# A gated mix of a long convolution and a token MLP: the convolution in two halves with a split transform, the shift filter on the matrix engine, one-pass gelu, and a list-scheduled instruction order

## The chip, the cores and the metric

The kernel runs on one core of one Trainium2 chip. A core has engines that run side by side: TensorE for matmuls (PE; its weight loads are PEld), VectorE (DVE), ScalarE (ACT), GpSimd (POOL) and SyncE (SP), which here issues most of the DMA transfers. Each engine takes its instructions in the order given: in the run in stated order below, DVE stood for 51.6 us at one operation with later ones ready behind it. Matmul results land in PSUM, and in both kernels ACT carries them to SBUF, which is called an eviction here.

The metric is the device time of one execution in microseconds. All runs compared below are of the fast state, unless it is said otherwise; executions of one kernel agree within about 1%.

## The reference, cut to what matters

```python
# S = 2048 tokens, D = 640 channels, F = 1536, bf16 inputs
g = sigmoid((q * gate_w).sum(-1))                   # one gate a token
# part A: shift filter of 4 taps, then a causal convolution as long as the sequence
k_shift = sum(k delayed by j tokens * shift_k[:, j] for j in 0..3)
kv = k_shift * v
y  = irfft(rfft(pad(kv)) * rfft(pad(ssm_k)))[:S] + kv * ssm_D
a  = q * y
# part B: MLP over the token axis
h  = layernorm(q)
u  = gelu_tanh(h.T @ w1 + b1)                       # 2048 -> 1536
b  = (u @ w2 + b2).T                                # 1536 -> 2048
return g * a + (1 - g) * b
```

Both MLP products are 2048 x 1536 x 640. They stay 384 matmuls of 320 columns each in both kernels.

## The kernel before: the parts that the argument touches

The convolution is cut into four blocks of 512 tokens. Each block of the filter and of kv is transformed by matmuls with cosine and sine tables, real and imaginary part by itself, and the output spectrum of block m sums the products of all pairs of blocks j and m - j, which makes ten pairs.

```python
def fwd_units(src_tile, blk0, dst_fn, scale):        # 8 units a block
    for c, Tt in ((0, Tc), (1, Ts)):                 # cosine, sine
        for kb in range(NB):                         # 4 frequency tiles
            # ... two PSUM banks, 4 + 4 matmuls of 320 columns, one eviction on ACT

def kv_tile(t, e_="DVE"):                            # shift filter of one tile of 128 tokens
    tt(e_, ka, ks[:, 0, :], shkb[:, 0, :], ALU.mult)
    tt(e_, k0, ks[:, 1, :], shkb[:, 1, :], ALU.mult)
    # ... eight operations of 640 elements in all, on VectorE

def product_pair(j, m_, slot):                       # one of ten pairs, 6 or 8 operations of 2560
    tt(e_, t0, Ar, Wr, ALU.mult)
    tt(e_, t1, As, Ws, ALU.mult)
    tt(e_, Zr, Zr, t0, ALU.add)
    # ...

def b1_set(s_, ...):                                 # gelu by a polynomial and a sigmoid
    evac(ubs[:, fi, :], q0 + fi, ACT.Identity, bias=b1c, scale=1.0)
    evac(sqs[:, fi, :], q0 + fi, ACT.Square, bias=b1cs, scale=GC)
    # ...
    stt(ge, sqf, sqf, 1.0, ubf, ALU.add, ALU.mult)                 # DVE
    gelu_sig.append(lambda ...: act(sgf, sqf, ACT.Sigmoid, scale=GS2))
    gelu_mul.append(lambda ...: tt(ge, gT[...], sgf, ubf, ALU.mult))   # DVE
```

Its order was laid out by hand: shift-filter tiles between the sets of the first MLP product, and the last product pairs between blocks of the second.

Of the kernel before, what the change touches and what calls it, by code (L numbers as in the profile page):

```python
# [17 lines left out]
class _Tracker:  # L18
# [31 lines left out]
    def regions(self, ap):  # L50
# [24 lines left out]
        if outer and nouter <= 64:  # L75
            idxs = [0] * len(outer)
            for _ in range(nouter):
                o = rem
                for (st, ct), i in zip(outer, idxs):
                    o += st * i  # L80
                lo = o
                hi = o
                for st, ct in inner:
                    ext = st * (ct - 1)
                    if ext < 0:
                        lo += ext
                    else:
                        hi += ext
                hi += 1
                assert lo >= 0 and hi <= rowsize, (name, apl, off, rowsize)  # L90
                res.append((space, p0, p1, base + lo * esize, base + hi * esize))
                for d in range(len(outer) - 1, -1, -1):
                    idxs[d] += 1
                    if idxs[d] < outer[d][1]:
                        break
                    idxs[d] = 0
        else:
# [10 lines left out]
            res.append((space, p0, p1, base + lo * esize, base + hi * esize))  # L108
        return res

# [161 lines left out]
    def mm(self, ps_ap, lhsT, rhs, start, stop, final_val):  # L272
        reads = [lhsT, rhs]
        acc_r = []
        for a in reads:
# [9 lines left out]
        ins = self.nc.tensor.matmul(ps_ap, lhsT=lhsT, rhs=rhs, start=start, stop=stop)  # L285
# [3 lines left out]
        if start:  # L289
            for r in ps_regs:  # L290
                self.add_record(r, "W", src)
        if stop:
# [7 lines left out]
def _chunks(D, maxc=512):  # L300
    n = (D + maxc - 1) // maxc
    base = D // n
    rem = D % n
    out = []
    lo = 0
    for i in range(n):
        w = base + (1 if i < rem else 0)
        out.append((lo, w))
        lo += w
    return out  # L310
# [12 lines left out]
NASP = 4  # L323
NUB = 4
NEPI = 7
KV_PRE = 3
KV_CHUNKS = (3, 3, 3, 2, 2, 0)
TM_PAIR_US = 9.5
TM_PAIR0_US = 7.0
TM_BLOCK_PE_US = 8.8  # L330
TM_PH4_LAG_US = -5.0
TM_EPI_US = 0.8
TM_EPI_LAG_BLOCKS = 2
EPI_ENG = "DVE"
OUT_ENG = "SP"


def _build(nc, A_q, A_k, A_v, A_shift_k, A_ssm_k, A_ssm_D, B_x, B_w1, B_b1, B_w2, B_b2, gate_w, out):
    Bsz, S, D = A_q.shape
    assert Bsz == 1  # L340
    F = B_w1.shape[1]
    KS = A_shift_k.shape[1]
    assert KS == 4
    P = 4
    n = S // P
    assert n % 128 == 0 and S % 128 == 0 and F % 128 == 0
    NB = n // 128
    NT = S // 128
    FT = F // 128
    L = 2 * n - 1  # L350
    N2 = 2 * n
    IB = 2 * NB
    DCH = _chunks(D, 512)
    NDC = len(DCH)
    assert NDC <= 2
    FS = 2 if FT % 2 == 0 else 1
    NSETS = FT // FS

    xd = A_q
    kd = A_k  # L360
    vd = A_v

    with ExitStack() as es:
        clk = {}
        for e in ENGS:
            clk[e] = es.enter_context(nc.semaphore(f"clk_{e}"))
        T = _Tracker(nc, clk)

        def dsem(name):
            s = es.enter_context(nc.semaphore(f"d_{name}"))  # L370
            T.add_dma_sem(name, s)

        for nm in ["const", "shk", "b", "out"]:
            dsem(nm)
        for i in range(NT):
            dsem(f"x{i}")
        for i in range(NEPI):
            dsem(f"xe{i}")
        for i in range(2):
            dsem(f"k{i}")  # L380
            dsem(f"v{i}")
            dsem(f"w2{i}")
        for i in range(2):
            for j in range(2):
                dsem(f"w1{i}{j}")
                dsem(f"w1p{i}{j}")
        for i in range(P):
            dsem(f"wT{i}")

        pp = []  # L390
        for i in range(4):
            h = es.enter_context(nc.psum_tensor(f"pp{i}", [128, 1024], F32))
            T.reg_psum(h, nc.lookup_mloc(h).bank)
            pp.append(h)

        def pview(q, widths):
            w = widths[0]
            assert all(x == w for x in widths)
            if len(widths) == 1:
                return pp[q][:, 0:w]  # L400
            return pp[q][:, :].rearrange("p (c f) -> p c f", c=2)[:, :, 0:w]

        base0 = (nc.sbuf_base + 63) // 64 * 64
        top = nc.sbuf_top
        cur = [base0]

        def alloc(name, shape, dtype):
# [3 lines left out]
            off = cur[0]  # L411
            cur[0] = (off + size + 63) // 64 * 64
            assert off + size <= top, f"SBUF overflow allocating {name}: {off}+{size} > {top}"
# [3 lines left out]

        gwb = alloc("gwb", [128, D], BF16)
        stats = alloc("stats", [128, NT, 6 * NDC], F32)
        mv = alloc("mv", [128, NT, 2], F32)  # L420
        rstd = alloc("rstd", [128, NT], F32)
        nbias = alloc("nbias", [128, NT], F32)
        gpre = alloc("gpre", [128, NT], F32)
        gg = alloc("gg", [128, NT], F32)
        omg = alloc("omg", [128, NT], F32)
        c2 = alloc("c2", [128, NT], F32)
        b2f = alloc("b2f", [128, NT], F32)
        b1f = alloc("b1f", [128, FT], F32)
        b1s = alloc("b1s", [128, FT], F32)
        b2t = alloc("b2t", [128, NT], BF16)  # L430
        b1t = alloc("b1t", [128, FT], BF16)
        cst = alloc("cst", [128, 4], F32)
        acol_i = alloc("acol_i", [128, NB], I32)
        acol_f = alloc("acol_f", [128, NB], F32)
        vpe = alloc("vpe", [128, NT], F32)
        Dall = alloc("Dall", [128, D], BF16)
        Tc = alloc("Tc", [128, NB, N2], BF16)
        Ts = alloc("Ts", [128, NB, N2], BF16)
        gT = alloc("gT", [128, FT, D], BF16)
        wT_base = cur[0]  # L440
        wT = alloc("wT", [128, NT, D], BF16)
        kv_base = cur[0]
        kvall = alloc("kvall", [128, NT, D], BF16)
        persist_end = cur[0]
        cur[0] = kv_base
        xb = [alloc(f"xb{i}", [128, D], BF16) for i in range(NT)]
        assert cur[0] <= persist_end
        cur[0] = persist_end

        cur[0] = wT_base  # L450
        w2b = [alloc(f"w2b{i}", [128, FT, 256], BF16) for i in range(2)]
        xe = [alloc(f"xe{i}", [128, D], BF16) for i in range(NEPI)]
        cur[0] = max(cur[0], kv_base)
        o1 = [alloc(f"o1_{i}", [128, D], BF16) for i in range(NEPI)]
        cg = [alloc(f"cg_{i}", [128, D], BF16) for i in range(NEPI)]
        osb = [alloc(f"osb_{i}", [128, D], BF16) for i in range(2)]
        end4 = cur[0]
        union_base = max(persist_end, end4)

        cur[0] = union_base  # L460
        Wsp = alloc("Wsp", [128, P, 2, NB, D], BF16)
        r1_base = cur[0]

        cur[0] = r1_base
        Zsp = alloc("Zsp", [128, P, 2, NB, D], BF16)
        Asp = [alloc(f"Asp{i}", [128, 2, NB, D], BF16) for i in range(NASP)]
        ptmp = [alloc(f"ptmp{i}", [128, NB, D], BF16) for i in range(2)]
        end2 = cur[0]

        cur[0] = r1_base  # L470
        hall_base = cur[0]
        hall = alloc("hall", [128, NT, D], BF16)
        shkb = alloc("shkb", [128, KS, D], BF16)
        kacc = alloc("kacc", [128, D], BF16)
        ktmp = [alloc(f"ktmp{i}", [128, D], BF16) for i in range(2)]
        junk = ktmp[0]
        late_base = cur[0]
        w1b = [alloc(f"w1b{i}", [128, NT, FS * 128], BF16) for i in range(2)]
        kb_ = [alloc(f"kb{i}", [128, KS, D], BF16) for i in range(2)]
        vb = [alloc(f"vb{i}", [128, D], BF16) for i in range(2)]  # L480
        ub = [alloc(f"ub{i}", [128, FS, D], BF16) for i in range(NUB)]
        save_cur = cur[0]
        cur[0] = cur[0] - (FS * D * 2 + 63) // 64 * 64
        assert KS * D * 2 <= FS * D * 2 or True
        shk2 = alloc("shk2", [128, D, KS], BF16)
        cur[0] = max(save_cur, cur[0])
        gsq = [alloc(f"gsq{i}", [128, FS, D], BF16) for i in range(NUB)]
        NLATE_MAX = 2
        n_early = max(0, NSETS - NLATE_MAX)
        gsg_e = [alloc(f"gsg{i}", [128, FS, D], BF16) for i in range(min(3, NSETS))]  # L490
        gsg = [gsg_e[i % len(gsg_e)] for i in range(NSETS)]
        end1 = cur[0]
        cur[0] = late_base
        brow_i = alloc("brow_i", [128, n], I32)
        prod_h = alloc("prod_h", [128, NB, n], I32)
        tbA = [alloc(f"tbA{i}", [128, NB, 128], I32) for i in range(2)]
        tbB = [alloc(f"tbB{i}", [128, NB, 128], I32) for i in range(2)]
        tbC = [alloc(f"tbC{i}", [128, NB, 128], I32) for i in range(2)]
        tbD = [alloc(f"tbD{i}", [128, NB, 128], F32) for i in range(2)]
        tbE = [alloc(f"tbE{i}", [128, NB, 128], F32) for i in range(2)]  # L500
# [600 lines left out]
```

## Time and profile before

| | before |
|---|---|
| time, median | 293.62 us (3 runs, 292.29 to 295.8) |
| span of the profiled run | 291.6 us |
| PE busy | 247.7 us, 1728 matmuls |
| DVE busy | 239.6 us |
| ACT busy | 113.5 us |

These lines are from the page of the kernel before: busy time by engine with its share of the span, then the busy tenths of PE, DVE and ACT in 40 equal slices (9 is 90% or more), and the shares of the chain of waits that ended last.

```profile
PE 247.7 (85%) x1728; PEld 172.4 (59%) x1728; DVE 239.6 (82%) x375; ACT 113.5 (39%) x153; POOL 35.0 (12%) x72
...
PE   0056989999999999767999999999999999059993
DVE  8999999096699899999999999997269999974211
ACT  2335569981235550746566323222222222002221
...
PE 44%; DVE 40%; DMA 5%; POOL 4%; issue 3%; ACT 3%; ACTq 0%; DVEq 0%; POOLq 0%
```

Neither engine is full over the whole span, but in almost every slice one of them is. That is what a chain of 44% PE and 40% DVE means: they take turns. The table of windows of before names the stages (stretch in us, its length, then busy time of PE, PEld, DVE, ACT and POOL, granted clock, DMA share, GB/s):

```profile
71.00:100.00 29.00, 29.00 (x216) 20.86 (x214) 23.13 (x48) 11.55 (x16) 0.00 (x0) 1.00 0.91 269
100.00:137.00 37.00, 30.12 (x205) 20.13 (x204) 35.86 (x70) 18.54 (x25) 0.00 (x0) 0.95 0.73 214
137.00:205.00 68.00, 68.00 (x490) 48.43 (x489) 65.49 (x57) 26.49 (x37) 0.00 (x0) 0.97 0.14 41
205.00:260.00 55.00, 44.41 (x319) 31.15 (x318) 47.24 (x41) 9.91 (x12) 0.00 (x0) 0.91 0.25 74
260.00:292.00 32.00, 27.18 (x186) 18.69 (x183) 7.33 (x16) 5.83 (x7) 0.00 (x0) 0.93 0.25 81
```

The last row is TensorE alone: 27.2 us of matmuls with DVE busy for 7.3. In the rows before it DVE is busy for 80 to 97% of the time. Two groups of before say with what (engine, operation, tiles, shapes, count, then busy us in total and mean ns of one, then idle time before):

```profile
L506 DVE TENSOR_TENSOR Zsp<-Zsp,ptmp_124 128x2560 bf16<-128x2560 bf16 x16 | 23.8, 1487 | 0.2
...
L506 DVE TENSOR_TENSOR kacc<-kacc,ktmp_128 128x640 bf16<-128x640 bf16 x32 | 15.6, 488 | 0.6
```

The first is part of the pair products, the second part of the shift filter (128 operations of some 0.49 us, 64 us together; the last of the eight for each tile is the product with v).

### The profile page before, as it was taken

What the parts mean: (1) busy time and instruction counts of PE and PEld (TensorE: products, weight loads), DVE (VectorE), ACT (ScalarE), POOL (GpSimd) and SP (SyncE); (2) the same over time, 40 slices, a digit from 0 to 9 for tenths busy, and PEclk for the clock granted to TensorE, in tenths of its full rate; (3) what the DMA queues carried; (4) which work ended last, traced back from release to release, by engine and by line L of the source; (5) the groups of instructions that cost most, each with busy time, mean ns of one, the idle gap of its engine ahead of it and who ended that gap; (6) DMA issues with size and microseconds to landing.
All of it is one profiled execution on the core that took longest, in us unless ns stands there. A gap on an engine that the chain in (4) does not pass through costs nothing.

```text
span 291.6 us, 4373 instructions
## 1 busy us (share of the span) xinstructions
PE 247.7 (85%) x1728; PEld 172.4 (59%) x1728; DVE 239.6 (82%) x375; ACT 113.5 (39%) x153; POOL 35.0 (12%) x72
## 2 busy tenths in 40 slices
PE   0056989999999999767999999999999999059993
PEld 0033657777777776434677777777777776026772
DVE  8999999096699899999999999997269999974211
ACT  2335569981235550746566323222222222002221
POOL 1223988820000000000000000000000000000000
PEclk9997899999999999979899999999999999658999
DMA  6979697347799986692000054002932300016100
GB/s 141 305 145 136 149 164 222 112 143 210 207 287 320 306 259 204 189 276 69 0 2 0 0 169 117 2 0 71 277 118 58 119 3 0 0 44 199 70 22 22
DMA packets 54530, 37.44 MB, mean 128 GB/s; under 512 B 16756, under 2 KB 53870, under 8 KB 54510
## 3 DMA queue, kind: packets, MB, share of 16 engines
q1 hardware_dynamic: 45614, 30.88, 38.2%
q10 hardware_dynamic: 8320, 4.19, 5.3%
q0 software_dynamic: 576, 2.10, 3.5%
q8 instruction: 13, 0.21, 0.3%
q14 instruction: 7, 0.06, 0.1%
HBM read 31.92 MB, written 2.62 MB: 118 GB/s over the span
## 4 chain that ended last, share of the span: by engine, by line
PE 44%; DVE 40%; DMA 5%; POOL 4%; issue 3%; ACT 3%; ACTq 0%; DVEq 0%; POOLq 0%
PE pp L285 44%; DVE Zsp L506 8%; DVE kacc L506 7%; DVE ktmp_128 L506 4%; DVE ptmp_124 L506 3%; DVE ptmp_123 L506 3%; DMA out_dram<-osb_116 3%; DMA kb_132<-in_A_k_dram 2%; DVE ktmp_129 L506 2%; DVE kvall L506 2%; DVE tbC_155 L506 1%; DVE tbC_154 L506 1%; DVE stats L626 1%; DVE gT L506 1%; POOL vpe L511 1%
## 5 line engine op out<-in xcount | busy, mean ns | idle before, releaser
L285 PE MATMUL pp<-Zsp,Tc 128*128 128x320 bf16 x224 | 41.3, 309 | 7.4 <-DVE Zsp L506 7.4
L285 PE MATMUL pp<-Zsp,Ts 128*128 128x320 bf16 x224 | 41.1, 308 | 3.2 <-DVE Zsp L506 3.2
L285 PE MATMUL pp<-wT,Tc 128*128 128x320 bf16 x128 | 21.4, 330 | 20.5 <-DMA wT<-in_A_ssm_k_dram 17.7
L285 PEld LDWEIGHTS pp<-Zsp,Tc 128*128 128x128 bf16 x224 | 22.4, 100 | 17.0 <-DVE Zsp L506 7.7
L285 PEld LDWEIGHTS pp<-Zsp,Ts 128*128 128x128 bf16 x224 | 22.4, 100 | 13.0 <-DVE Zsp L506 3.8
L285 PEld LDWEIGHTS pp<-wT,Tc 128*128 128x128 bf16 x128 | 13.3, 106 | 27.5 <-issue 17.7
L285 PE MATMUL pp<-gT,w2b_93 128*128 128x320 bf16 x192 | 27.2, 300 | 0.0
L285 PE MATMUL pp<-gT,w2b_92 128*128 128x320 bf16 x192 | 27.2, 299 | 0.0
L285 PE MATMUL pp<-hall,w1b_130 128*128 128x320 bf16 x192 | 26.6, 300 | 0.0
L285 PE MATMUL pp<-hall,w1b_131 128*128 128x320 bf16 x192 | 26.6, 299 | 0.0
L546 ACT ACTIVATE Wsp<-pp 128x640 bf16<-128x640 f32 x32 | 21.8, 738 | 8.7 <-PE pp L285 8.5
L285 PE MATMUL pp<-kvall,Ts 128*128 128x320 bf16 x128 | 20.8, 326 | 5.3 <-ACT Asp_119 L546 3.1
L506 DVE TENSOR_TENSOR Zsp<-Zsp,ptmp_124 128x2560 bf16<-128x2560 bf16 x16 | 23.8, 1487 | 0.2
L506 DVE TENSOR_TENSOR Zsp<-Zsp,ptmp_123 128x2560 bf16<-128x2560 bf16 x16 | 23.7, 1484 | 0.0
L285 PEld LDWEIGHTS pp<-gT,w2b_92 128*128 128x128 bf16 x192 | 18.8, 98 | 7.4
L285 PEld LDWEIGHTS pp<-gT,w2b_93 128*128 128x128 bf16 x192 | 18.8, 98 | 7.3
L285 PEld LDWEIGHTS pp<-hall,w1b_130 128*128 128x128 bf16 x192 | 18.8, 98 | 7.3
L285 PEld LDWEIGHTS pp<-hall,w1b_131 128*128 128x128 bf16 x192 | 18.8, 98 | 7.3
L285 PE MATMUL pp<-wT,Ts 128*128 128x320 bf16 x128 | 19.9, 319 | 1.4 <-ACT Wsp L546 1.4
L285 PE MATMUL pp<-kvall,Tc 128*128 128x320 bf16 x128 | 19.3, 309 | 1.6 <-ACT gsq_142 L546 1.5
L285 PEld LDWEIGHTS pp<-kvall,Ts 128*128 128x128 bf16 x128 | 13.2, 105 | 12.2 <-ACT Asp_119 L546 3.8
L285 PEld LDWEIGHTS pp<-wT,Ts 128*128 128x128 bf16 x128 | 13.2, 104 | 7.8 <-ACT Wsp L546 1.8
(198 smaller groups left out, 356.6 us busy)
## 6 DMA issues: line engine op xcount, KB each, us to landing
kb_133<-in_A_k_dram SPq DMA_DIRECT2D x32, 160.0 KB, 2.7
kb_132<-in_A_k_dram SPq DMA_DIRECT2D x29, 160.0 KB
w2b_92<-in_B_w_dram SPq DMA_DIRECT2D x4, 768.0 KB, 4.9
w2b_93<-in_B_w_dram SPq DMA_DIRECT2D x4, 768.0 KB, 5.5
w1b_130<-in_B_w_dram ACTq DMA_DIRECT2D x4, 512.0 KB, 5.9
w1b_131<-in_B_w_dram ACTq DMA_DIRECT2D x4, 512.0 KB, 5.9
vb_134<-in_A_v_dram SPq DMA_DIRECT2D x8, 160.0 KB, 3.6
vb_135<-in_A_v_dram SPq DMA_DIRECT2D x8, 160.0 KB, 3.3
```

The costliest lines, as they stand in the source:

```text
L285: ins = self.nc.tensor.matmul(ps_ap, lhsT=lhsT, rhs=rhs, start=start, stop=stop)
L506: return T.op(eng, lambda e: e.tensor_tensor(out_, in0, in1, op), [in0, in1], [out_])
L511: return e.tensor_scalar(out_, in0, s1, None, op0=op0)
L546: return T.op("ACT", lambda e: e.activation(out_, in_, func, **kw), rr, [out_])
L626: T.op("DVE", (lambda ci, dlo, dw: lambda e: e.bn_stats(stats[:, t, ci * 6:(ci + 1) * 6], xs[:, dlo:dlo + dw]))(ci, dlo, dw), [xs[:, dlo:d ...
```

## The change

The change wants less work on both engines of the chain, and an order that keeps both busy.

- The convolution works on two halves of 1024 tokens. Each half is split by token index modulo 4 into four phases, which are transformed with small tables and then combined on DVE by additions and subtractions (`mixing`, `invmix`). That leaves 256 forward and 128 inverse matmuls where before had 512 and 448, and six large products in place of ten pairs. The filter is loaded as it lies and transposed on TensorE.
- The shift filter is 140 matmuls with diagonal tables (`DG`), on k loaded transposed.
- Gelu is one ACT instruction for a tile.
- The gate's row sums move from DVE to a wide DVE product and 16 ACT sums.
- Every operation is put into a list with an estimated duration, and a list scheduler in the kernel's builder writes the order. At each moment of its model it gives each engine the ready operation that was stated first, or that has a lower priority number.

```diff
-            tt(e_, ka, ks[:, 0, :], shkb[:, 0, :], ALU.mult)      # shift filter: 8 such a tile
+                    for q in range(4):
+                        items.append(((lambda s, b=b, q=q: s[:, 512 * b + 128 * q:512 * b + 512]),
+                                      V(KT[h], base + q, [[4, 128]]), DG[:, db, 0:4 - q, :]..., q == 0, False))
...
-            stt(ge, sqf, sqf, 1.0, ubf, ALU.add, ALU.mult)
-            gelu_sig.append(...); gelu_mul.append(...)
+            act(GT[:, ft, :]..., two, ACT.Gelu_apprx_tanh, bias=b1f[:, ft:ft + 1], vt=vt, prio=0, name="gelu")
...
+        def mixing(R, Th, Ts):                                    # 8 operations of 2560, four times
+            tt("DVE", sl(Th, Ts), sl(R, 0), sl(R, 2), ALU.add)
+            tt("DVE", sl(R, 0), sl(R, 0), sl(R, 2), ALU.subtract)
+            # ...
+        def product(dst, a, v):                                   # six times
+            tt("DVE", P2(T0), P2(a), P2(v), ALU.mult)             # 5120 elements
+            tt("DVE", P2(T1), P2(a), P2(v, True), ALU.mult)
+            tt("DVE", H(dst, 0), H(T0, 0), H(T0, 1), ALU.subtract)
+            tt("DVE", H(dst, 1), H(T1, 0), H(T1, 1), ALU.add)
...
+            tt("DVE", xg[:, :, :], X[:, hk, :, :], V(gwb, 0, [[0, 4], [1, D]]), ALU.mult)
+            for p in range(4):
+                act(xg[:, p, :], xg[:, p, :], ACT.Copy, acc=gpre[:, 4 * hk + p:4 * hk + p + 1], name="ga")
...
-        while pending:                                            # hand-made order
-            j, m_ = pending.pop(0)
-            product_pair(j, m_, j % NASP)
-            emit_ready_quads()
+        y1(0); y1(1)                                              # products of the second half
+        Z1 = invmix(A1[0], A1[1], C3a, None, None)
+        inverse(1, Z1)
+        product(A0[0], A0[0], V0[0])
+        product(A0[1], A0[1], V0[1])
+        Z0 = invmix(A0[0], A0[1], (SS, 0), None, None)
+        inverse(0, Z0)
+        SC.run()                                                  # list scheduling
+        SC.emit()
```

## The prediction

> **What bounds it now.** Busy table: span 291.6 us, PE 247.7 (85%), DVE 239.6 (82%), ACT 113.5. The chain of waits is 44% PE and 40% DVE, in turns. By the table of windows: until 40 us DVE builds tables and statistics while PE waits 17.7 us for the transposed filter; 71 to 137 DVE is nearly full with the shift filter (eight 640-wide operations a tile, 0.49 us each); 137 to 205 both are full; 216 to 259 is pure DVE products (2560 wide, 1.40 to 1.49 us each); 259 to 287 is pure PE (188 matmuls, 28.2 us).
>
> **PE.** Before: 1728 matmuls of 320 columns. After: 1152 (forward 256, MLP 768, inverse 128), 140 shift matmuls (40,960 columns) and 114 small transposes. The trace's dense rate is 137 to 140 ns per 320 columns (224 in 30.6 us; 488 in 68.2 us). Estimates: 1152 x 0.14 = 161; shift 18; transposes 114 x 0.1 = 11. Sum 190 us, some 52 below before's 242 at that rate.
>
> **DVE.** Estimates from 1.40 to 1.49 us per 2560 elements: four forward mixings of eight operations 46; kv, spectrum-merge and gate products 18; products 56; two inverse mixings 23; statistics (0.41 x 32 + 0.2 x 16) 16; tables 8; normalising 5; epilogue (32 x 0.49) 15. Sum about 187 us, 53 below before. Gone are 128 shift operations (63 us), the gelu polynomial and most of the pair products; new are the mixings.
>
> **ACT.** 64 spectrum evictions (0.71 us), 16 filter evictions, 16 gate sums, 12 shift evictions, 12 gelus, 32 in the tail: about 130 us. It should not bind overall, but paces the first 50 us: 0.71 per eviction exceeds 0.56 for its four matmuls. Table loads stay few: the Trainium skill (ScalarE: Activation LUTs, What ACT_TABLE_LOAD costs) gives 1283 ns; the trace has 1283.
>
> **DMA.** 37 MB becomes about 28; transposed loads (about 145 GB/s in their slices, plain ones about 300) now carry k, needed later than the filter was.
>
> **Critical path.** Both engines of the chain lose about 52 us, and the MLP overlaps the DVE chain. Estimated DVE chain: filter spectra mixed near 66, signal spectra 104, products 142, inverse mixing 154, second half 190, then 12 us of inverse matmuls, epilogue and store: about 203. PE: MLP from about 50 us, when weights and normalised x exist, 155 us left: 205. Add 5 to 8% for stalls of a static order, throttled stretches (clock 0.91 to 0.97 late) and the start.
>
> **Prediction:** 220 us, range 203 to 242; faster by over 2% 0.96, within 2% 0.02, slower 0.02.
>
> **Right or wrong shows as:** PE busy 190 to 215, DVE 178 to 195, ACT 120 to 140; PE over 90% busy from 55 us to near the end; DVE gaps under 30 us in total; a final stretch with DVE idle under 15 us (28 before); no wait over 5 us for w1 or v.
>
> **What would make it wrong.** (1) The second MLP product and the shift read weights with element step 4. The skill (TensorE: Matmul & The Clock Gate, Weight-path perf modes) allows fast weight load to a step of 1,024, so I assume no penalty; before has none to compare. If LDWEIGHTS exceeds 140 ns, 384 matmuls lengthen. (2) k transposes delaying v and w1. (3) An order built from estimated durations: head-of-line stalls on PE and ACT. (4) Reversed-half operands losing the [...]rate, adding 30 us or more to DVE.

## The result and the profile after

The kernel after takes 217.03 us (median of 4 runs, 216.88 to 217.26) against 293.08 for before in the same measurements. The ratio is 0.7395, interval 0.7361 to 0.7428. A ratio is the mean time of one kernel's fast runs over that of the other's of the same rounds, so not quite the ratio of the medians. The profile of after:

```profile
PE 192.9 (90%) x1406; PEld 139.7 (65%) x1406; DVE 184.5 (86%) x197; ACT 119.3 (55%) x181; POOL 18.0 (8%) x22
...
PE   0579944999879899999999999999999999999993
DVE  8999599998999258966999999999997669998650
ACT  2798999799984996395213112113314472323751
...
PE 72%; ACT 23%; DMA 2%; issue 0%; DVE 0%
```

PE lost 54.8 us of busy time (247.7 to 192.9), DVE 55.1 (239.6 to 184.5) and ACT gained 5.8. The sum of PE and DVE busy time over the span was 1.67 before and is 1.75 now. The turns are gone: from the 15th slice on PE is full, and DVE is nearly full beside it in most slices. The start has a new owner: ACT holds 23% of the chain, all but 0.9 us of it before 73 us. The table of windows of after (columns as above):

```profile
0.00:73.00 73.00, 54.32 (x385) 36.12 (x386) 66.33 (x105) 61.98 (x104) 18.04 (x22) 0.93 0.73 204
73.00:212.00 139.00, 138.59 (x1022) 103.61 (x1022) 117.64 (x91) 56.76 (x78) 0.00 (x0) 1.00 0.30 98
```

PE is busy for 138.6 of the 139 us from 73 to 212, and for 54.3 of the first 73. Near its end the chain of waits reads so, in order of time (start, duration, what):

```profile
70.81 1.28 ACT L641
72.10 0.80 ACT GT L641
72.91 0.05 issue
72.95 138.65 PE pp L291 x1022
```

One reads "the kernel is PE-bound for two thirds of its span" there. The experiments below show that this is only half of it.

Two smaller readings answer questions of the prediction. These are groups of after: the weight loads of the first MLP product, whose weights lie side by side, and of the second, whose weights are read with an element step of 4; then one of the reversed-half products.

```profile
L291 PEld LDWEIGHTS pp<-X,ring_80 128*128 128x128 bf16 x256 | 24.9, 98 | 11.5 <-issue 1.8 <-ACT C_85 L641 0.2
...
L291 PEld LDWEIGHTS pp<-GT,W_1_99 128*128 128x128 bf16 x192 | 21.7, 113 | 4.4
...
L603 DVE TENSOR_TENSOR tm_101<-C_84,SS 128x5120 bf16<-128x5120 bf16 x1 | 2.8, 2818 | 0.0
```

The step of 4 costs 15 ns a load (113 against 98), and the matmul stream hardly feels it: 128 matmuls of the first product in a row took 17.55 us and 96 of the second 13.20 us, 137 and 138 ns each. The reversed-half products keep the rate of the other operations (5120 elements in 2.82 us, twice the 2560 in 1.41 of back-to-back operations).

One DVE operation stands out. These are the timelines of POOL and of DVE in after, around 10 us (start, duration, engine, what); the later instances of the same DVE operation took 1.48 us each:

```profile
9.67 4.46 POOL L603 TENSOR_TENSOR DG<-ident,shk 128x2560 bf16<-128x2560 bf16 x1 [8.07 <-DMA shk<-in_A_shift_k_dram]
...
10.68 0.44 DVE L790 BATCH_NORM_STATS2 stats<-X 128x6 f32<-128x320 bf16 x1
11.04 4.43 DVE L603 TENSOR_TENSOR xg<-X,gwb 128x2560 bf16<-128x2560 bf16 x1
```

While POOL builds the shift table, the DVE operation with one input runs at its usual 0.44 us, but the one with two inputs ends only 1.3 us after POOL does. The Trainium skill (GPSIMD Engine Reference, 1. Specifications) says that POOL shares its SBUF interfaces with VectorE and names two SBUF inputs as a case of contention. The trace agrees, and gives its size: 3 us here, practically a full stop. The last run shows the other direction too: there a POOL copy of 20 columns took 7.16 us, from 29.56 to 36.72 us, while DVE ran two-input operations end to end until 36.66 us. In after the same copy took 0.60 us.

### The profile page after: what moved, and what is told of

Its sections match the earlier page's. It is cut to its first block, busy times and chain, and to the rows that moved or that the text cites. A ratio compares the mean times of both kernels' runs of the same rounds, so it can differ in the third digit from the quotient of the medians.

```text
span 215.2 us, 3363 instructions
## 1 busy us (share of the span) xinstructions
PE 192.9 (90%) x1406; PEld 139.7 (65%) x1406; DVE 184.5 (86%) x197; ACT 119.3 (55%) x181; POOL 18.0 (8%) x22
## 4 chain that ended last, share of the span: by engine, by line
PE 72%; ACT 23%; DMA 2%; issue 0%; DVE 0%
PE pp L291 72%; ACT xg L641 5%; ACT C_82 L641 4%; ACT C_83 L641 3%; ACT wT L641 3%; DMA ssm<-in_A_ssm_k_dram 2%; ACT FTB L641 2%; ACT L641 2%; ACT ksh_94 L641 2%; ACT GTB L641 1%; ACT C_84 L641 1%; ACT ksh_95 L641 0%; ACT O_100 L641 0%; ACT GT L641 0%; DVE O_100 L603 0%
## 5 line engine op out<-in xcount | busy, mean ns | idle before, releaser
L291 PE MATMUL pp<-X,ring_80 128*128 128x320 bf16 x256 | 35.6, 299 | 1.5 <-ACT ksh_95 L641 1.5
L641 ACT ACTIVATE O_100<-pp,c_66,omg 128x640 bf16<-128x640 f32 x16 | 14.2, 885 | 35.0 <-PE pp L291 35.0
L291 PEld LDWEIGHTS pp<-X,ring_80 128*128 128x128 bf16 x256 | 24.9, 98 | 11.5 <-issue 1.8
L291 PE MATMUL pp<-GT,W_1_99 128*128 128x320 bf16 x192 | 26.9, 299 | 0.0
L291 PE MATMUL pp<-GT,W_0_98 128*128 128x320 bf16 x192 | 26.4, 299 | 0.0
L291 PEld LDWEIGHTS pp<-GT,W_1_99 128*128 128x128 bf16 x192 | 21.7, 113 | 4.4
L291 PEld LDWEIGHTS pp<-GT,W_0_98 128*128 128x128 bf16 x192 | 21.8, 113 | 4.3
L291 PE MATMUL pp<-wT,FTB 128*128 128x320 bf16 x128 | 21.8, 335 | 0.0
L291 PE MATMUL pp<-ident,ssm 128*128 128x128 bf16 x80 | 9.5, 287 | 12.9 <-ACT wT L641 6.8
L291 PEld LDWEIGHTS pp<-wT,FTB 128*128 128x128 bf16 x128 | 12.4, 109 | 9.0 <-ACT C_82 L641 1.9
L291 PE MATMUL pp<-X,ring_81 128*128 128x320 bf16 x128 | 17.7, 299 | 0.0
L291 PEld LDWEIGHTS pp<-X,ring_81 128*128 128x128 bf16 x128 | 12.5, 98 | 4.8
L790 DVE BATCH_NORM_STATS2 stats<-X 128x6 f32<-128x320 bf16 x32 | 13.5, 461 | 0.0
L603 DVE TENSOR_TENSOR C_83<-C_84 128x2560 bf16<-128x2560 bf16 x4 | 5.9, 1490 | 7.2 <-ACT C_84 L641 7.2
L641 ACT ACTIVATE xg<-xg 128x640 bf16<-128x640 bf16 x16 | 11.8, 804 | 0.0
L603 DVE TENSOR_TENSOR C_84<-C_85 128x2560 bf16<-128x2560 bf16 x5 | 7.4, 1490 | 3.8 <-ACT C_85 L641 3.8
```

The costliest lines, as they stand in the source:

```text
L291: ins = self.nc.tensor.matmul(ps_ap, lhsT=lhsT, rhs=rhs, start=start, stop=stop, skip_group_check=True)
L603: return SC.add(eng, d, lambda s: T.op(eng, lambda e: e.tensor_tensor(o, a, b, op), [a, b], [o]), [a, b], [o], prio=prio, name="tt")
L641: return T.op("ACT", lambda e: e.activation(o, src, func, **kw), rr + [src], ww)
L790: SC.add("DVE", 0.42, (lambda o, i: lambda s: T.op("DVE", lambda e: e.bn_stats(o, i), [i], [o]))(o, i), [i], [o])
```

## The experiments

Theory A, which the sums of the prediction and the chain of waits of after suggest: the gain is the work taken off both engines, with the order worth a smaller part; after 73 us PE alone sets the pace. (The prediction itself put the DVE chain at 203 us and PE at 205, two nearly equal paths.) Rival B: the order is the larger part, or DVE binds as much as PE. Ratios to after are formed from two ratios to before; the control run, the kernel after unchanged, gave 217.03 us and 0.7375. Except for the stated orders, every variant of after was list-scheduled anew, so its order can differ beyond the edit shown.

> The kernel after unchanged, as control of this call: 217 us, within 0.5%.

### The same operations in stated order

```diff
-        SC.run()
+        SC.program_order()      # operations as stated, PSUM slots dealt in turn
         SC.emit()
```

> The kernel after, with the same operations issued in the order in which the program states them (convolution, first MLP product, second MLP product, products and inverse) instead of the list-scheduled one; PSUM slots dealt in turn. Theory A (most of the gain is work removed from TensorE and VectorE, the order is worth a smaller part): 230 to 250 us, busy times unchanged at about 193 and 185, PE idle up by 15 to 30 us, mostly in the first 90 us. Rival B (the gain is overlap brought by the list-scheduled order): 265 us or more.

Measured: 274.41 us, ratio to before 0.930 (0.926 to 0.933). The rival's number: with the same operations, the program runs 57 us longer. The run changes the dealing of PSUM slots together with the order. Its mean PE clock was also lower, 0.87 to 0.88 in the fast executions (0.97 to 0.98 in after), so a part of the 57 us can be slower matmuls beside the waits. Its profile fell in a slow execution (span 277.4 us, PE busy 201.7, DVE 189.9), so only its large waits are read here, from its view of waits:

```profile
DVE cgb L611 <- ACT cgb L649: 51.6, 1, 51.6
...
PE pp L291 <- DVE C L611: 25.8, 1, 25.8
```

The first is a wait for an order and not for data. The program states the first inverse transform, with its DVE epilogue, before the last two products. PE reaches that transform only after the whole MLP, so DVE stands for 51.6 us at the epilogue with the products ready behind it. Then it works alone, and PE waits 25.8 us. Three moves of statements, each on top of the one before, test how much of the loss is of this kind.

```diff
 # first move
-        inverse(1, Z1)
         ...
         Z0 = invmix(A0[0], A0[1], (SS, 0), None, None)
+        inverse(1, Z1)
         inverse(0, Z0)
 # second move: m1(ft) is one tile of the first MLP product
         for hk in range(2): kv(hk)
+        for ft in range(4): m1(ft)
         # ... first signal transform, kv(2), kv(3)
+        m1(4); m1(5)
         # ... second signal transform
 # third move: the table DG stated at the start; kv(0), kv(1) stated before the mixing of the second filter half
```

> The program-order variant with one move: the second half's products and inverse mixing are stated before the first inverse transform, so VectorE need not wait for that transform's epilogue, which TensorE reaches only after the whole MLP. In the program-order run VectorE idled 51.6 us there and then worked 36 us alone. Theory A (that one inversion costs the tail): 244 to 254 us, VectorE's idle stretch gone, last matmuls dense. Rival B (the tail is bound otherwise): 268 us or more.

Measured: 245.29 us (0.833). The inversion at the tail cost 29 us, as theory A of this run had it. DVE still idles there for 19.6 us of the 51.6, but PE is full through that time.

> The same with a second move: six of the twelve tiles of the first MLP product stated earlier, four before the first signal transform and two before the second, where TensorE waited for VectorE in the program-order run. Theory A (the rest of the loss of the program order is TensorE idling before the MLP): 218 to 232 us. Rival B (the list-scheduled order wins by many small choices): 238 us or more.

Measured: 234.37 us (0.7965). It gained 11 us and falls between the two theories, 218 to 232 and 238 or more; PE still waited 16.8 us for the table DG, which POOL made late because the operations stated before it waited for DVE.

> The program order with the two moves and a third: the table for the shift filter is stated at the start, and the two gate products of the first half before the mixing of the second filter half, so the first signal transform can start while VectorE mixes. In the run with two moves VectorE idled 14.3 us and 10.0 us waiting for signal spectra, and PE 16.8 us for the table. Theory A (a hand order with three moves does all that the list scheduler did): 214 to 223 us. Rival B: stays above 226 us, the list scheduler's small choices matter.

Measured: 231.68 us (0.7859). This falls to rival B. The wait for DG is gone and another has its place, from its view of waits:

```profile
PE pp L291 <- POOL KT L659: 15.8, 1, 15.8
```

That is a memset of 20 columns which takes 0.11 us, stated behind POOL operations that wait for DVE. Each move opened the next head of line. The list scheduler's order is 57 us better than the stated order and 14.7 us better than the best of these hand orders. The hand orders keep the slots dealt in turn, so how much of the 14.7 us is the slots is not shown, nor how a fourth move would do.

### The gelu, taken alone in both kernels

The one-pass gelu was put into before alone, and the old gelu was put back into after.

```diff
 # in before
-                evac(ubs[:, fi, :], q0 + fi, ACT.Identity, bias=b1c, scale=1.0)
-                evac(sqs[:, fi, :], q0 + fi, ACT.Square, bias=b1cs, scale=GC)
+                evac(gT[:, fb0 + fi, :], q0 + fi, ACT.Gelu_apprx_tanh, bias=b1c, scale=1.0)
-            stt(...); gelu_sig.append(...); gelu_mul.append(...)
 # in after
-            act(GT[:, ft, :]..., two, ACT.Gelu_apprx_tanh, bias=b1f[...], ...)
+            act(GT[:, ft, :]..., two, ACT.Identity, bias=b1f[...], ...)
+            act(sq..., two, ACT.Square, bias=b1s[...], scale=math.sqrt(0.044715), ...)
+            stt("DVE", sq[:, :], sq[:, :], 1.0, GT[:, ft, :], ALU.add, ALU.mult)
+            act(sq[:, :], sq[:, :], ACT.Sigmoid, ...)
+            tt("DVE", GT[:, ft, :], GT[:, ft, :], sq[:, :], ALU.mult)
```

> The kernel before, with the one-pass gelu alone. DVE busy falls by about 13 us, ACT by about 17. Theory A (DVE is on the chain from 71 to 137 us, where the gelu sits): 279 to 287 us. Rival B (PE, busy throughout 71 to 100, paces that stretch): within 1% of before, 290 us or more.

Measured: 282.66 us, 0.9576. Theory A's number: DVE busy fell from 239.6 to 227.1 and the time by 12.4 us, about one for one. The edit also took 11.7 us off ACT (113.5 to 101.8), so that DVE was the one that counted is argued from the chain of waits of before and not shown by this run.

> The kernel after, with the gelu of before put back: two evictions, two VectorE operations and a sigmoid for each of 12 tiles (about 13 us more on DVE, 17 us more on ACT by the durations of before's trace). Theory A (from 73 us on only the matmul stream binds, DVE and ACT have room there): 216 to 221 us, DVE busy about 198, ACT about 137. Rival B (DVE binds as much as PE): 226 us or more.

Measured: 226.68 us (0.7676; over after 0.7676 / 0.7395 = 1.038). Rival B: 9.7 us more, in a kernel whose chain of waits said 72% PE. Here is one window of this run, and below it the same window of after:

```profile
140.00:160.00 20.00, 15.53 (x94) 10.64 (x95) 20.00 (x16) 7.28 (x10) 0.00 (x0) 0.83 0.43 145
140.00:160.00 20.00, 20.00 (x150) 16.49 (x148) 20.00 (x12) 5.22 (x6) 0.00 (x0) 1.00 0.64 216
```

DVE is at 20.00 of 20.00 us in both, so it had no room for more in after either. What differs is PE: the gelu operations take their turn between DVE products of 2.8 us, PE waits for the tiles, is busy for 15.53 us in place of 20.00, and its clock is 0.83. This run had only two scratch tiles for the gelu, for want of SBUF, so part of its loss may be theirs.

### More DVE work, less PE work

Two runs weigh the two engines against each other without that doubt.

```diff
 # more DVE: one multiplication of each product twice
             tt("DVE", P2(T1), P2(a), P2(v, True), ALU.mult)
+            tt("DVE", P2(T1), P2(a), P2(v, True), ALU.mult)
 # less PE (wrong result on purpose): three of four phases in the first MLP product
-                for p in range(4):
+                for p in range(3):
```

> The kernel after with one multiplication of each of the six complex products done twice (six times 2.8 us, 17 us more DVE, all after 108 us, same result). The chain of waits of after is pure PE from 73 us to the end, DVE idle about 20 us in that time. Theory A (PE alone binds there): 221 us or less. Theory B (the DVE chain through products, inverse mixing and inverse is as long as the matmul stream, so the two bind together): 227 to 236 us.

Measured: 228.99 us (0.7776): 16.4 us more DVE busy time (200.9) cost 12.0 us. The chain of waits of this run ends so:

```profile
207.34 4.22 DVE C L603 x3
211.56 0.14 issue
211.70 10.64 PE pp L291 x64
```

The last 64 matmuls are the last inverse transforms, and they wait for the last inverse mixing, PE for 9.25 us.

> The kernel after with a quarter of the first MLP product left out (96 of 384 matmuls, 13 us less PE; wrong result on purpose). Theory A (PE alone binds after 73 us): 202 to 206 us. Theory B (PE and the DVE chain are of equal length, as the run with 17 us more DVE says, which cost 12): 210 to 217 us.

Measured: 213.15 us (0.7233; over after 0.7233 / 0.7375 = 0.981), with 96 matmuls left out: an estimated 13 us, and 9.8 us less PE busy time as measured (183.1). Only 3.9 us were seen in the time. That is under 2%, but clear of the spread (212.09 to 214.12 us against 216.93 to 218.24 of the control). Its chain of waits ends like that of the run with more DVE work:

```profile
192.31 4.21 DVE C L603 x3
196.53 0.14 issue
196.66 11.19 PE pp L291 x64
```

So theory B holds: the matmul stream and the chain of kv products, mixings, products, inverse mixings and inverse transforms end at nearly the same moment. The chain of waits follows only one of two paths of nearly equal length, and shows PE. PE fills in with matmuls of the MLP until the last mixing is done. The timelines of after show how much of these it had left: the last inverse mixing, the last inverse transforms, and then matmuls of the second MLP product.

```profile
195.58 2.89 DVE L603 TENSOR_TENSOR SS<-C_84,C_83 128x2560 bf16<-128x2560 bf16 x2
...
201.65 4.51 PE L291 MATMUL pp<-SS,GTB 128*128 128x320 bf16 x32
206.00 5.60 PE L291 MATMUL pp<-GT,W_1_99 128*128 128x320 bf16 x40
```

By this the DVE path was some 5.6 us shorter than the matmul stream. Both runs fit this: of 16.4 us more DVE work 4.4 did not show, and of 9.8 us less PE work the first 3.9 did.

### The shift filter back on VectorE

```diff
+                for j in range(4):                       # 1280-element halves
+                    src = kw[:, 3 + pa - j:5 + pa - j, :]
+                    # ... tt(mult) with the broadcast filter row, tt(add) into the sum
-                        # ... 35 matmuls a tile row with DG, three evictions
```

> The kernel after, with the shift filter back on VectorE (four products and three sums a tile row, 14 operations of 1280 elements, about 10.5 us for each of four tile rows, so 42 us more DVE; 140 matmuls, some 18 us of PE and 11 us of ACT less, and plain loads of overlapping rows in place of the transposed loads of k). Theory A (DVE is nearly as long as PE, so moving the shift to PE was worth its DVE time): DVE becomes the limit, 238 to 255 us, DVE busy 220 to 228, PE busy about 174. Rival B (DVE has slack, only the number of matmuls counts): 200 to 220 us.

Measured: 274.58 us (0.9317), outside what either theory said. My edit was at fault. One load of k for the first tile row covered 127 partitions, because the first partition has no earlier tokens. This is its line in the chain of waits; the weight tiles of the first MLP product were queued behind it, and PE waited 20.4 us for one:

```profile
18.65 47.97 DMA KW<-in_A_k_dram
```

It moved 1111 KB in 48 us, 24 GB/s; the 128-partition loads of 1120 KB took a median of 5.2 us to landing. The Trainium skill (DMA: Bandwidth & Descriptors, Why a DMA increments its semaphore by 16 and not by 1) has this very case: the number of DMA engines is the largest number up to 16 that divides the outer sizes, and "127 partitions" gives 1. The run agrees: from 28 to 40 us, with this transfer under way, the mean busy share of the 16 DMA engines was 0.07, about one of them. The repaired load:

```diff
-                dma(KW[0][1:128, :, :], ...)
+                dma(KW[0][:, 3:7, :], ...)
+                dma(KW[0][1:113, 0:3, :], ...)
+                dma(KW[0][113:128, 0:3, :], ...)
```

> The shift filter on VectorE again, with the load repaired that took 50 us in the first try (a transfer over 127 partitions, 1111 KB; now over 128, 112 and 15). Theory A (VectorE is nearly as long as TensorE, so its 42 us more bind): 236 to 256 us, DVE busy 220 to 228. Rival B (VectorE had slack and only the load was at fault): 222 us or less.

Measured: 262.02 us (0.8883), 45 us over after. DVE busy is 223.6, 39.1 more than in after, and PE busy 187.0, 5.9 less where I had expected some 18. Theory A was right that DVE binds, but the time is over its range: DVE also waited for spectra and loads (12.9 us for spectra, 5.5 for k), and at the end PE waited 18.0 us for the last mixing. Part of the 45 us is thus the order and the buffers of this variant rather than the 39 us of DVE work; the runs do not split it further. That PE's busy time fell less fits with its clock, 0.874 on average in place of 0.974; it was not followed further.

### The gate sums off ScalarE

```diff
-            tt("DVE", xg[:, :, :], X[:, hk, :, :], V(gwb, 0, [[0, 4], [1, D]]), ALU.mult)
             for p in range(4):
-                act(xg[:, p, :], xg[:, p, :], ACT.Copy, acc=gpre[...], name="ga")
+                stt("DVE", xg[:, p, :], X[:, hk, p, :], 1.0, gwb[:, :], ALU.mult, ALU.mult, acc=gpre[...])
```

> The kernel after with the gate's row sums as one VectorE operation with a sum a tile (16 of about 0.73 us) in place of one wide product and four ScalarE sums a tile row: ACT loses about 16 us, all before 59 us, DVE gains about 3. Theory A (evictions on ACT pace the first 60 us, PE waits there for wT evictions 6.8 us): 210 to 214 us. Rival B (DVE paces the start as much, or the DVE chain sets the end): 216 to 221 us.

Measured: 206.95 us (0.7022; over after 0.7022 / 0.7375 = 0.952), correct: the fastest kernel, and better than theory A said. Its busy times, and the end of its chain of waits:

```profile
PE 189.6 (92%) x1406; PEld 139.0 (68%) x1406; DVE 189.8 (92%) x225; ACT 107.9 (53%) x149; POOL 34.3 (17%) x22
```

```profile
33.01 139.84 PE pp L291 x1036
...
187.60 4.22 DVE C L603 x3
191.82 0.14 issue
191.95 8.87 PE pp L291 x64
```

In after, the gate sums (xg) stood in ACT's queue ahead of evictions (wT) that PE waited for, as its chain of waits shows:

```profile
29.02 2.81 ACT xg L641 x8
31.83 2.37 ACT wT L641 x4
```

Over the whole chain of after these sums make 11.4 us. Without them the unbroken stream of matmuls starts at 33 us (at 73 in after), and the first matmul of the MLP comes at 51.9 us (at 61.6 in after). The PE clock also stays up, 0.999 on average: in after it was 0.66 from 30 to 40 us, where PE waited for evictions. PE lost 3.3 us of busy time with the same matmuls and 6.7 us of idle time (215.2 - 192.9 = 22.3 in after, 205.2 - 189.6 = 15.6 here), 10.0 us together. DVE took 5.3 us more and the time still fell. My reading, not tested by itself, is that these operations sit at the start, where the later DVE chain gains from an earlier start of the transforms. Now the DVE chain visibly sets the end: the last 64 matmuls wait for the last mixing, as in the run with more DVE work.

## Why the prediction was right, and where its reasons were not

- Total: 220 us predicted, 217.03 measured.
- The sums held. PE 190 to 215, measured 192.9. DVE 178 to 195, measured 184.5. ACT 120 to 140, measured 119.3, a hair below. They were built from durations of the trace of before, and the same kinds of operation took about the same time in after (2560 elements on DVE 1.48 us, 320 columns on PE 137 to 138 ns).
- That "the MLP overlaps the DVE chain", taken for granted in one clause, decides how much of the gain is had. The stated order of the same operations takes 274.41 us, only 20 us better than before, so 57 of the 76 us hang on the order (with its slots and clock). My first expectation of 230 to 250 us for it was wrong: the two-engine sums say only what is possible. The prediction's picture, a DVE chain of about 203 us and PE of 205, was right: two nearly equal paths, and the runs with 16.4 us more DVE (+12.0 us) and 9.8 us less PE (-3.9 us) confirm it. Its milestones ran late: the two inverse mixings ended at 165.4 and 198.5 us, and not at 154 and 190.
- The allowance of 5 to 8% was named for stalls of a static order, throttled stretches and the start. Only the start and its throttled stretch used it: the MLP began at 61.6 us and not at 50, and after 73 us PE stood for 0.4 us in 139. The allowance was not worked out from anything, so that a start 11.6 us late came to just about it is luck. The cause was in one clause of the prediction, that ACT "paces the first 50 us", and I had not thought through that the gate sums stood before the evictions; the run without them gave 10 us.
- "PE over 90% busy from 55 us": 86% from 55 to 70 (12.94 of 15 us), full from 73. "DVE gaps under 30 us": 30.7 (215.2 - 184.5). "No wait over 5 us for w1 or v": none; PE's only wait for DMA of that size was 5.7 us for the filter at the very start. "A final stretch with DVE idle under 15 us": DVE worked to the end, and its longest wait in the last 20 us was 2.8 us.
- Of the four dangers, the weight step of 4 cost 15 ns a load and no time that shows, the transposed loads of k delayed nothing that PE waited for, the static order stalled in its first 73 us (the gate sums ahead of the evictions) and not after, and the reversed halves kept their rate.
- How much of the gain is the smaller transform itself is not shown by a run; it was not undone alone. The counts and busy times of the two traces are all that is known of it: 384 transform matmuls in place of 960. Nor was before list-scheduled, which is a rival for a part of the gain: its order may have left time to win. It can't be all of it: 1728 matmuls at the 137 to 140 ns of before's dense stretches are an estimated 237 to 242 us of PE, so at least some 20 us of the gain needed fewer matmuls. The parts do not add up either: with two paths of nearly equal length, taking one part back costs much of its time or more (gelu 9.7 us for 13.4 us of DVE work, shift filter 45 us for 39.1, order 57 us).

## What to carry to other kernels

Add up the work of each engine from measured durations, and then ask for the order separately: the same operations took 274 us in one order and 217 in another, and a queue that stands behind an operation waiting for another engine's far later work is the pattern to look for. When a chain of waits shows one engine only, test the other by giving it a little more work: two paths of nearly equal length look like one. And look at small low-value operations (gate sums, a 20-column memset, a table on GpSimd) that stand early in a queue ahead of what a busy engine waits for; moving 16 of them off ScalarE gave 4.8%.

## What the Trainium skill lacked or had wrong

- TensorE: Matmul & The Clock Gate (Weight-path perf modes) gives no time for weights read with a step. Here 128 columns took 98 ns side by side and 113 ns at a step of 4.
- TensorE: Matmul & The Clock Gate (Back-to-back issue gap) states a sustained spacing of about 131 ns for N=512. The dense streams here have 320 columns and already took 137 to 140 ns each, which is nearer to the page's other formula, N / 2.4 + 2.5 = 135.8. No run here has such a stream of 512 columns.
- ScalarE: Activation LUTs (What ACT_TABLE_LOAD costs) counts 2.66 us for a switch of tables, 1283 ns of it the load. The load took 1.28 us in every trace, and at 70.81 us of after the next instruction began 1.29 us after the load's start: no further drain was seen there.
- ScalarE: Activation LUTs has no time for reading an activation's sum out: it was a separate instruction of 0.19 to 0.36 us after each of the 16 sums.
